# Rows of tokens scattered straight to their expert's place in DRAM, in a fused attention, FFN and top-1 MoE kernel

## The chip, the cores and the metric

One core of a Trainium2 chip runs the whole kernel. The metric is device time in microseconds (us) from start to end of one execution; lower is better. The engines are named as in the profile: PE (matmul; PEld is its weight load), DVE (vector), ACT (scalar), POOL (GpSimd) and SP (which here only issues DMAs and reads registers). ACT and POOL issue some DMAs too. All DMAs run on the core's 16 DMA engines.

## What is computed

Three stages, each feeding the next. 1536 tokens, 512 features.

```
def reference(**kwargs):
    attn_out = _attn_ref(**attn_kwargs)          # 2 x 8 heads x 768 x 64, causal band of 96 + 8 global keys, ALiBi-like bias
    x = np.ascontiguousarray(attn_out.transpose(0, 2, 1, 3)).reshape(B * S, H * D)
    x = _moe_ref(x=x, **moe_kwargs)              # h = x @ w_in (512x2048); (h * sigmoid(h)) @ w_out
    return _moe2_ref(x=x, **moe2_kwargs)

def _moe2_ref(x, w_gate, w_output_gate, w1, w2):
    logits = x @ w_gate                          # 8 experts
    e_idx = np.argmax(logits, axis=1)
    ...                                          # gate_w: softmax probability of the chosen expert
    eom = 1.0 / (1.0 + np.exp(-(x @ w_output_gate)))
    for e in range(E):
        mask = e_idx == e
        h = np.maximum(x[mask] @ w1[e], 0.0)     # 512x1024
        ye = h @ w2[e]                           # 1024x512
        out[mask] = gate_w[mask, None] * eom[mask, e, None] * ye
    return out.astype(np.float32)
```

## The kernel before

The program is ordered by hand: the Python code writes the instructions in the order in which each engine's queue gets them, and each engine runs its own queue in order. P is 128.

**Attention.** The 12 blocks n of 128 queries (6 per batch entry) with 4 head pairs each give 48 slots s. The first 24 slots (n = 0 to 5) run in `slot_b`, fully in float32: per slot `emit_qk` (PE, scores of the next slot), `emit_tb` (DVE, adds the bias and takes the maximum, one instruction per head), `emit_exp` (ACT), `emit_dg` (DVE reciprocals, POOL diagonal matrices), `emit_tr` (PE, the transpose with the scaling, `tp`), `emit_cp` (copy from PSUM, DVE or ACT) and `emit_px` (PE, times v). From slot 8 on a piece of weight decoding (`dec_op`, DVE) stands in each slot. After the last head pair of a block, `emit_xx` calls `put_xt` (L241 to L246): ACT copies the block's result from PSUM to the tile `xT` (rounded, the high part) and DVE writes the difference, the low part, at once. That DVE instruction stands at the end of a slot, ahead of the next slot's `emit_tb`. Slots 0 to 19 and a little more run alone at the program's start; the last of them run inside the first FFN chunk. The loads of the scores' inputs (`ring`) are issued by ACT some four slots ahead, those of v (`vpr`) and of the packed FFN weights (`wiraw`, `woraw`, `wraw`) by SP. Slots 24 to 47 run in `slot`, inside FFN chunks 1 to 3: there POOL makes the low halves `hl` (L176), SP transposes them by DMA (`pT`, L179), and PE multiplies them with v (`pv`, L222).

**FFN.** The tokens go through in five chunks CH=[[0,1],[2],[3],[4],[5]] of token pairs u (256 tokens each), 16 steps each over the hidden features. `s1_mm` (L315) is the first product, `s2_mm` (L335 to L337) the second, two steps later. The low half of the second weight is stored to DRAM in chunk 0 (`wlo_d`, L301) and read again per step in the later chunks (`wolr`, L304).

**Gate.** After a chunk, `s2_ev` puts the 256 rows into `xr` (128 x 2 x 528; 512 features and 16 more columns). `gate1`, `gate2`, `gate3` stand in a list that `run_gates` works off, one entry per FFN step. `gate3(u)` computes each token's place `di` in its expert's list, scatters the token's number there (POOL, L416: two indirect DMAs of 128 x 4 bytes), computes the row's output factor into columns 512 to 527 (DVE reciprocal, L423), and SP stores the 256 rows in token order to the DRAM tensor `XS` (L424). There are two index lists in DRAM, `IX[0]` and, for the last 128 tokens alone, `IX[1]`; `ix_init` fills both with the number of a spare row at the start of chunk 1 (L360 to L368).

**Experts.** `order` ranks the experts by their number of tokens. Expert p of the ranking takes its WIN[p] first places (352 down to 192). The first 128 rows of expert 0 are computed early, in the last FFN chunk: SP reads their index list (`ei`, L494) and POOL gathers the rows (`ex`, `exg`, L499), three indirect DMAs. After the gate, `moe2` runs p = 0 to 7 with 8 steps f each. `load_i` (SP) reads both index lists (`ixt`), `min_i` (DVE) merges them, `load_x` (POOL, L592) gathers the rows (`xw`), `prep_x` transposes them on PE (`xm`, L600); the loop's weights come as `qr` (SP, L480), are split by ACT, DVE and POOL into `uq`, and `put` (POOL, L575) scatters the results to the output, one indirect DMA of 128 rows of 2 KB each.

## Time and profile before

| | us |
|---|---|
| median of 3 runs | 644.12 (639.51 to 645.3) |
| profiled execution, whole | 638.47 |
| its span in the trace | 636.7 |
| PE busy | 594.6 (93%) |
| DVE, ACT, POOL busy | 387.0, 303.3, 208.6 |
| moved by DMA | 99.01 MB (11.61 MB written to DRAM) |
| share of the chain that ended last | PE 69%, DMA 10%, DVE 8%, issue 6%, ACT 4% |

The profiled execution is 0.9% below the median; 1.8 us of its time lie outside the span. Engines' times are busy times within the span. The chain is followed back from the last instruction: each piece is work, or a DMA, that the next piece waited for. PE is busy for most of the span; its idle time and the stretches at a lower granted clock are the rest of the chain.

### The profile page before, as it was taken

The numbers are of one execution on the slowest core, as the hardware profiler recorded it, in microseconds if no ns is written. First come the engines' busy times: TensorE is split into PE (matmuls) and PEld (weight loads), VectorE is DVE, ScalarE is ACT, GpSimd is POOL, SyncE is SP. The second block draws the span as 40 slices with busy tenths as digits, with TensorE's granted clock in tenths as the row PEclk, the third lists the DMA queues.
The fourth block names the chain that finished last, engine by engine and source line by source line (L and its number), as shares of the span: only waits on it lengthen the run. The fifth ranks groups of instructions, "written<-read, shape, count | busy, mean of one in ns | idle before, by whom it ended". The sixth has DMA issues, their size and how long they took to land.

```text
span 636.7 us, 12051 instructions
## 1 busy us (share of the span) xinstructions
PE 594.6 (93%) x4054; PEld 504.1 (79%) x4054; DVE 387.0 (61%) x1060; ACT 303.3 (48%) x802; POOL 208.6 (33%) x248
## 2 busy tenths in 40 slices
PE   2898999999999799999999999998999999999994
PEld 1566788888888588888889998786888888888883
DVE  3577679999546544645463344754835569777740
ACT  5467533343353335343432233744553666676741
POOL 3467614444212242222221001323432434343311
PEclk9999999999999889999999999999799999999998
DMA  7143706774348976485437339715847287578500
GB/s 252 44 129 126 215 34 188 227 218 147 114 142 92 172 160 182 99 165 147 116 91 129 99 80 192 274 35 174 292 148 237 85 283 235 177 244 261 180 18 19
DMA packets 83673, 99.01 MB, mean 156 GB/s; under 512 B 35547, under 2 KB 49883, under 8 KB 83602
## 3 DMA queue, kind: packets, MB, share of 16 engines
q1 hardware_dynamic: 76850, 86.78, 50.0%
q0 software_dynamic: 3312, 8.22, 3.9%
q10 hardware_dynamic: 3440, 3.15, 1.6%
q8 instruction: 34, 0.56, 0.4%
q14 instruction: 37, 0.30, 0.2%
HBM read 82.01 MB, written 11.61 MB: 147 GB/s over the span
## 4 chain that ended last, share of the span: by engine, by line
PE 69%; DMA 10%; DVE 8%; issue 6%; ACT 4%; POOL 2%; SPq 1%; POOLq 0%; DVEq 0%; ACTq 0%
PE s L315 16%; PE s L335 5%; PE s L336 5%; PE s L337 5%; PE h L612 4%; PE tp L193 4%; PE h L618 4%; PE qkp L150 4%; PE y L635 4%; PE y L637 4%; PE y L636 4%; DMA pT<-hl 2%; PE h L613 2%; PE pv L222 2%; PE gl L380 2%
## 5 line engine op out<-in xcount | busy, mean ns | idle before, releaser
L315 PEld LDWEIGHTS s<-xT,wi 128*128 128x128 f32 x1152 | 149.3, 193 | 14.3 <-DVE g L324 7.1
L315 PE MATMUL s<-xT,wi 128*128 128x256 f32 x1152 | 154.1, 286 | 2.6 <-DVE xT L246 1.4
L320 DVE SCALAR_TENSOR_TENSOR s<-u,s 128x256 f32<-128x256 f32 x96 | 39.7, 426 | 88.9 <-ACT u L319 88.9
L319 ACT ACTIVATE u<-s 128x256 f32<-128x256 f32 x96 | 35.2, 380 | 119.5 <-PE s L315 118.9
L335 PE MATMUL s<-woh,g 128*128 128x512 f32 x192 | 79.5, 414 | 0.0
L486 DVE TENSOR_TENSOR uq<-qr,uq 128x512 fp32r<-128x512 f32 x87 | 71.0, 837 | 9.1 <-ACT uq L485 4.4
L336 PE MATMUL s<-woh,g 128*128 128x512 f32 x192 | 76.0, 396 | 0.0
L485 ACT ACTIVATE uq<-qr 128x512 fp32r<-128x512 f32 x112 | 66.7, 626 | 8.3 <-DMA qr<-in_w_dram 7.2
L324 DVE TENSOR_TENSOR g<-s,g 128x256 fp32r<-128x256 f32 x96 | 39.3, 422 | 31.6 <-ACT g L323 28.5
L635 PE MATMUL y<-uq,hh 128*128 128x512 f32 (+6 forms) x136 | 55.7, 409 | 0.0
L323 ACT ACTIVATE g<-s 128x256 fp32r<-128x256 f32 x96 | 35.6, 379 | 40.4 <-DVE s L320 39.4
L637 PE MATMUL y<-uq,hh 128*128 128x512 f32 (+6 forms) x136 | 54.0, 397 | 0.0
L636 PE MATMUL y<-uq,hh 128*128 128x512 f32 (+6 forms) x136 | 53.9, 396 | 0.0
L486 POOL TENSOR_TENSOR uq<-qr,uq 128x512 fp32r<-128x512 f32 x25 | 33.0, 1329 | 52.6 <-ACT uq L485 52.5
L169 ACT ACTIVATE t<-t,mx 128x256 f32<-128x256 f32 (+1 forms) x96 | 45.8, 480 | 6.1 <-DVE mx L162 4.2
L150 PE MATMUL qkp<-ring 64*128 64x256 f32 (+1 forms) x192 | 35.8, 448 | 13.2 <-DMA ring<-in_qk_dram 12.6
L628 DVE SCALAR_TENSOR_TENSOR hh<-h,hh 128x224 fp32r<-128x224 f32 (+6 forms) x64 | 25.3, 395 | 32.8 <-ACT hh L627 29.9
L627 ACT ACTIVATE hh<-h 128x224 fp32r<-128x224 f32 (+6 forms) x64 | 23.2, 363 | 43.4 <-DVE h L625 21.6
L335 PEld LDWEIGHTS s<-woh,g 128*128 128x128 f32 x192 | 36.3, 189 | 7.1 <-ACT u L319 2.0
L337 PE MATMUL s<-wolr,g 128*128 128x512 f32 x128 | 40.5, 398 | 0.0
L336 PEld LDWEIGHTS s<-woh,g 128*128 128x128 f32 x192 | 36.4, 190 | 5.0
L416 POOL DMA_INDIRECT ix<-tok,gdi x12 | 12.4, 1030 | 84.9 <-DVE gsm L420 43.1
(217 smaller groups left out, 1096.7 us busy)
## 6 DMA issues: line engine op xcount, KB each, us to landing
qr<-in_w_dram SPq DMA_DIRECT2D x128, 256.0 KB
wolr<-wlo_d SPq DMA_DIRECT2D x64, 256.0 KB
wiraw<-in_w_in_dram SPq DMA_DIRECT2D x16, 512.0 KB
wraw<-in_w_out_dram SPq DMA_DIRECT2D x13, 512.0 KB
wlo_d<-wol SPq DMA_DIRECT2D x16, 256.0 KB
xs<-xr SPq DMA_DIRECT2D x6, 528.0 KB
ring<-in_qk_dram SPq DMA_DIRECT2D x12, 256.0 KB
ring<-in_qk_dram ACTq DMA_DIRECT2D x10, 256.0 KB
```

The source lines that it names most:

```text
L150: T.matmul(q[:,sl],w[:,z,1],w[:,z:z+1,0] if i==0 else w[:,0:3:2,0] if z==0 else w[:,z-1:z+1,0],start=True,stop=True)
L169: A.activation(out=t[:,j,:ce],in_=t[:,j,:ce],func=AF.Exp,scale=0.125,bias=mx[n][:,h:h+1],accum_out=ss[n][:,h:h+1])
L315: T.matmul(t,w[:,ww,kc,:],x[:,xx,kc,:],start=(k==0),stop=(k==11)); k+=1
L320: V.scalar_tensor_tensor(out=t,in0=u,scalar=1.0,in1=t,op0=ALU.add,op1=ALU.mult)
L335: T.matmul(o,g[u][:,0,sl],wh,start=(f==0),stop=False)
L336: T.matmul(o,g[u][:,1,sl],wh,start=False,stop=False)
L337: else: T.matmul(o,g[u][:,0,sl],wl,start=False,stop=(f==FB-1))
L485: A.activation(out=t[:,0],in_=r,func=AF.Copy)
L486: (G if (i%2 if pool is None else pool) else V).tensor_tensor(out=t[:,1],in0=r,in1=t[:,0],op=ALU.subtract)
L635: T.matmul(o,g[:,0,sl],w[:,0],start=(f==0),stop=False)
L636: T.matmul(o,g[:,1,sl],w[:,0],start=False,stop=False)
L637: T.matmul(o,g[:,0,sl],w[:,1],start=False,stop=(f==7))
```

## The change

- The DRAM tensor `XE` (8 x 1536 rows of 528 floats) replaces `XS` and both index lists. `gate3` writes the token's number into column 513 of its row (POOL copy) and scatters 128 whole rows (2112 bytes each) to their places by an indirect DMA (`gate4(u,0)`). The other 128 rows (`gate4(u,1)`) are an entry of their own in the gate list. All scatters write one tensor, so each waits until the one before it has landed.
- The places that no token takes must hold zeros and the spare number: `rows_init` makes a tile `zr` (POOL), `rows_clear` stores it three times over per expert, eight DMAs of 128 x 3 x 528 floats (811 KB each, 6.5 MB in all), issued by SP after slots 4, 6, ... 18.
- The experts' rows are read by plain SP loads (`load_x`, `xw<-xe`; for the early rows `ex` and `exg`; for expert 0's factors and numbers `xtail`). The index loads, their merging and all 20 gathers by POOL are gone.
- The low part of `xT` for blocks n = 0 to 3 is put in a list (`xlow`) and issued in the next slot, after that slot's reciprocals.
- At the start of `moe2` SP issued the last `xs<-xr`, two `ixt` loads, read the experts' order, two more `ixt` loads, then the `qr` loads; now it reads the order, then issues three `xw<-xe`, `xtail<-xe` and the `qr` loads.
- `run_gates` works off two entries at two places and has one more call in `moe2`, since the list is longer.

```diff
-    XS=dr.tile([NTOK+1,XW],F32,name="xs"); IX=[dr.tile([NE*CAP,1],I32,name=f"ix{k}") for k in range(2)]
+    FAC=512; TOK=513; WROWS=(WIN[0]+P-1)//P*P
+    XE=dr.tile([NE*CAP,XW],F32,name="xe")
...
     def emit_xx(n):
-        put_xt(n,pvt[n])
+        put_xt(n,pvt[n],xlow if 4*(n+2)<SB else None)
...
-    def put_xt(n,m):
+    def put_xt(n,m,later=None):
...
         A.activation(out=sl[:,0],in_=m,func=AF.Copy)
-        V.tensor_tensor(out=sl[:,1],in0=m,in1=sl[:,0],op=ALU.subtract)
+        def low(): V.tensor_tensor(out=sl[:,1],in0=m,in1=sl[:,0],op=ALU.subtract)
+        if later is None: low()
+        else: later.append(low)
...
+    def rows_init():
+        z=mp.tile([P,XW],F32,tag="xT",name="zr",bufs=3); zr.append(z)
         G.memset(z,0.0)
-        S.dma_start(XS[NTOK:NTOK+1,:],z)
+        G.memset(z[:,TOK:TOK+1].bitcast(I32),NTOK)
+    def rows_clear(e):
+        S.dma_start(XE[e*CAP:e*CAP+WROWS,:].rearrange("(a p) d -> p a d",p=P),zr[0][:,None,:].to_broadcast([P,WROWS//P,XW]))
...
-        for t in range(2):
-            n=2*u+t
-            G.indirect_dma_start(out=IX[n==NTT-1][:,:],out_offset=bass.IndirectOffsetOnAxis(ap=di[:,t:t+1],axis=0),in_=tok[:,n:n+1],...)
...
-        S.dma_start(XS[2*u*P:2*(u+1)*P,:].rearrange("(k p) d -> p k d",p=P),xr)
+        G.tensor_copy(xr[:,:,TOK].bitcast(I32),tok[:,2*u:2*u+2])
+        gdi[u]=di,xr
+        gate4(u,0)
+    def gate4(u,t):
+        di,xr=gdi[u]
+        G.indirect_dma_start(out=XE[:,:],out_offset=bass.IndirectOffsetOnAxis(ap=di[:,t:t+1],axis=0),in_=xr[:,t,:],...)
...
+        x=m2['a'].tile([P,XW],F32,name="ex"); ea['x']=x
+        S.dma_start(x,XE[ds(e*CAP,P),:])
         g=mp.tile([P,2,XW],F32,tag="xT",name="exg",bufs=3); ea['xg']=g
+        S.dma_start(g,XE[ds(e*CAP+P,2*P),:].rearrange("(a p) d -> p a d",p=P))
...
+    def load_x(p):
+        small(p); e=ereg(p)
+        for j,n in tiles(p):
+            x=m2['b'].tile([P,XW],F32,tag="xw",name="xw",bufs=6); xwt[p,j]=x
+            S.dma_start(x,XE[ds(e*CAP+j*P,P),:])
...
-        load_i(0); load_i(1)
+        load_x(1); load_t(0)
...
             if o4: emit_px(n4,h4)
+            if xlow: xlow.pop()()
...
+            if s%2==0 and 4<=s<4+2*NE: rows_clear(s//2-2)
...
-                        for fn in (gate2,gate3): gq.append(lambda u=u,fn=fn: fn(u))
+                        for fn in (gate2,gate3,lambda u: gate4(u,1)): gq.append(lambda u=u,fn=fn: fn(u))
```

DVE, the end of block 1 in the attention slots, before. `xT<-px,xT` is the low part, `ISA t,mx` the bias and maximum of a head (a slot has two), `dct<-wiraw,dct` the weight decoding.

```order
L184 TENSOR_SCALAR ss<-ss 128x2
L185 RECIPROCAL ss<-ss 128x2
L246 TENSOR_TENSOR xT<-px,xT 128x4x128
L159 ISA t,mx<-qkp,tabs 128x256
L159 ISA mx 128x1
L271 SCALAR_TENSOR_TENSOR dct<-wiraw,dct 128x512
L159 ISA t,mx<-qkp,tabs 128x256
L159 ISA mx 128x1
L162 TENSOR_SCALAR mx<-mx 128x2
L184 TENSOR_SCALAR ss<-ss 128x2
L185 RECIPROCAL ss<-ss 128x2
```

The same place of the changed kernel:

```order
L186 RECIPROCAL ss<-ss 128x2
L160 ISA t,mx<-qkp,tabs 128x256
L160 ISA mx 128x1
L275 SCALAR_TENSOR_TENSOR dct<-wiraw,dct 128x512
L160 ISA t,mx<-qkp,tabs 128x256
L160 ISA mx 128x1
L163 TENSOR_SCALAR mx<-mx 128x2
L185 TENSOR_SCALAR ss<-ss 128x2
L186 RECIPROCAL ss<-ss 128x2
L248 TENSOR_TENSOR xT<-px,xT 128x4x128
L160 ISA t,mx<-qkp,tabs 128x256
```

The low part moved behind one whole slot's work of DVE; the next slot's first maximum no longer stands behind it.

POOL in chunk 1, the gates of u = 0 and 1, before (`hl` is the low half that SP transposes for PE, `vraw`, `vpr` the split of v):

```order
L176 TENSOR_TENSOR hl<-t,hl 128x2x128 x2
L416 DMA ix_73<-tok,gdi 12288x1 x2
L176 TENSOR_TENSOR hl<-t,hl 128x2x128
L129 TENSOR_TENSOR vraw<-vraw,vpr 128x512
L133 TENSOR_TENSOR vpr<-vraw,vpr 128x512
L176 TENSOR_TENSOR hl<-t,hl 128x2x256
L416 DMA ix_73<-tok,gdi 12288x1 x2
```

and in the changed kernel:

```order
L177 TENSOR_TENSOR hl<-t,hl 128x2x128 x2
L423 COPY xr<-tok 128x2
L429 DMA xe<-xr,gdi 12288x528
L177 TENSOR_TENSOR hl<-t,hl 128x2x128
L429 DMA xe<-xr,gdi 12288x528
L130 TENSOR_TENSOR vraw<-vraw,vpr 128x512
L134 TENSOR_TENSOR vpr<-vraw,vpr 128x512
L177 TENSOR_TENSOR hl<-t,hl 128x2x256 x2
L423 COPY xr<-tok 128x2
L429 DMA xe<-xr,gdi 12288x528
L177 TENSOR_TENSOR hl<-t,hl 128x2x256
L429 DMA xe<-xr,gdi 12288x528
```

One `hl` now stands between the two scatters of a pair; the second still waits for the first to land.

SP at the program's start in the changed kernel, with what each waits for (DMAHW: an earlier DMA that counts on the same semaphore has landed). The `xe<-zr` are the clears; before, the loads stood there without them, two of them in another order.

```order
L260 DMA wiraw<-in_w_in_dram 128x4x256
L370 DMA xe<-zr 128x3x528 [waits DMAHW0_49,Pool_49]
L260 DMA wiraw<-in_w_in_dram 128x4x256 [waits DMAHW2_49]
L370 DMA xe<-zr 128x3x528 [waits DMAHW4_49]
L124 DMA vpr<-in_v_dram 128x512 [waits DMAHW6_49]
L260 DMA wiraw<-in_w_in_dram 128x4x256 [waits DMAHW7_49]
L370 DMA xe<-zr 128x3x528 [waits DMAHW0_49]
L264 DMA woraw<-in_w_out_dram 128x1024 [waits DMAHW2_49]
L370 DMA xe<-zr 128x3x528 [waits DMAHW3_49]
L124 DMA vpr<-in_v_dram 128x512 [waits DMAHW7_49,PE_49,Pool_49]
```

Four clears stand ahead of the fourth v load, which waits for PE; the other four come after it.

## Rows read from the trace of the kernel before

**Rows 1.** The page: PE; the DMA engines' busy tenths in 40 slices.

```profile
PE 594.6 (93%) x4054; PEld 504.1 (79%) x4054; DVE 387.0 (61%) x1060; ACT 303.3 (48%) x802; POOL 208.6 (33%) x248
...
DMA  7143706774348976485437339715847287578500
```

**Rows 2.** Chain that ended last, attention slots: start us, us, what.

```profile
27.77 1.13 PE tp L193 x8
...
31.12 1.13 PE tp L193 x8
...
38.09 1.10 PE tp L193 x8
...
39.87 0.55 ACT xT L245
40.44 0.69 DVE xT L246
41.13 0.33 DVE t L159
...
41.62 1.13 PE tp L193 x8
```

**Rows 3.** Windows: length, busy PE, PEld, DVE, ACT, POOL, PEclk, DMA share, GB/s.

```profile
35.78:38.09 2.31, 2.31 (x21) 1.69 (x21) 1.73 (x9) 1.77 (x8) 1.22 (x3) 1.00 0.41 114
38.09:41.62 3.53, 2.31 (x21) 1.64 (x21) 1.75 (x7) 2.73 (x8) 2.70 (x7) 1.00 0.08 19
41.62:43.97 2.35, 2.35 (x21) 1.73 (x21) 2.28 (x10) 1.41 (x6) 1.55 (x3) 1.00 0.80 281
```

**Rows 4.** Chain at the start, the wait for the scores' inputs.

```profile
8.57 6.31 DMA ring<-in_qk_dram
```

**Rows 5.** DMA from 5 to 17 us: GB/s in 40 slices of 0.3 us.

```profile
GB/s 209 304 345 389 399 376 386 389 382 372 358 355 355 345 352 345 365 352 365 362 355 375 341 386 365 362 399 372 406 338 365 372 358 376 335 369 328 184 113 89
```

**Rows 6.** DMA from 193 to 207 us, slices of 0.35 us: busy tenths, GB/s.

```profile
DMA  0001960999990090009097947093903336525400
GB/s 26 3 0 23 219 133 2 355 362 362 284 66 6 18 18 0 0 0 24 0 12 6 18 30 23 24 35 29 41 0 6 18 29 71 71 53 199 176 7 0
```

**Rows 7.** DMA from 161 to 173 us, slices of 0.3 us, `wlo_d` stores: GB/s.

```profile
GB/s 328 369 382 260 27 0 0 150 410 307 7 0 0 0 0 0 27 0 0 0 0 0 0 314 382 191 7 7 0 0 0 0 0 0 0 0 0 362 389 294
```

**Rows 8.** Output scatters of line 575, 128 rows of 2 KB: landing.

```profile
DMA to landing us min/median/max: 2.8/2.8/3.7
```

**Rows 9.** Waits from 190 to 235 us: total, times, longest.

```profile
POOL ix L416 <- DVE gsm L394: 10.1, 1, 10.1
POOL ix L416 <- DMA ix<-tok,gdi: 9.5, 1, 9.5
...
PE pv L222 <- DMA pT<-hl: 4.6, 3, 2.8
```

**Rows 10.** Windows of FFN steps in chunk 1 (columns as in 3).

```profile
205.39:211.73 6.34, 4.73 (x38) 3.72 (x38) 5.37 (x18) 2.25 (x8) 4.41 (x5) 0.87 0.62 82
...
225.26:230.38 5.12, 5.12 (x44) 4.40 (x44) 1.27 (x5) 2.15 (x7) 1.43 (x2) 0.81 0.65 68
230.38:234.60 4.22, 4.12 (x43) 3.34 (x42) 2.81 (x11) 2.15 (x7) 1.17 (x2) 1.00 1.12 329
```

**Rows 11.** PE's waits for DMAs, 395 to 456 us.

```profile
PE xm L600 <- DMA xw<-xs,ixt: 3.0, 1, 3.0
PE em L514 <- DMA ex<-xs,ei: 1.6, 1, 1.6
```

**Rows 12.** Chain, from the last gate to expert 1's rows.

```profile
425.86 7.31 DMA ix<-tok,gdi
...
439.76 6.65 DMA xw<-xs,ixt
```

**Rows 13.** Windows behind that wait (columns as in 3).

```profile
445.00:450.00 5.00, 3.54 (x11) 2.80 (x12) 4.83 (x16) 2.86 (x7) 3.83 (x4) 0.57 0.99 378
450.00:455.00 5.00, 5.00 (x23) 4.43 (x22) 3.38 (x8) 2.45 (x6) 1.29 (x1) 0.75 0.78 200
```

More of the change, by code (lines that the diff above doesn't have):

```diff
@@ L359, in gate_consts @@
         S.dma_start(wgs,wg.rearrange("(k p) e -> p k e",p=P))
-    def ix_init():
-        n=NE*CAP//P
-        z=mp.tile([P,n],I32,tag="stage",name="zi",bufs=2)
-        G.memset(z,NTOK)
-        for x in IX: S.dma_start(x.rearrange("(p a) o -> p (a o)",p=P),z)
-        z=mp.tile([1,XW],F32,tag="stage",name="zx",bufs=2)
+    zr=[]
+    def rows_init():
+        z=mp.tile([P,XW],F32,tag="xT",name="zr",bufs=3); zr.append(z)
         G.memset(z,0.0)
-        S.dma_start(XS[NTOK:NTOK+1,:],z)
+        G.memset(z[:,TOK:TOK+1].bitcast(I32),NTOK)
+    def rows_clear(e):
+        S.dma_start(XE[e*CAP:e*CAP+WROWS,:].rearrange("(a p) d -> p a d",p=P),zr[0][:,None,:].to_broadcast([P,WROWS//P,XW]))
     def gate1(n):
@@ L423, in gate3 @@
         V.reciprocal(out=xr[:,:,512:XW],in_=s[:,:,29:30].to_broadcast([P,2,XW-512]))
-        S.dma_start(XS[2*u*P:2*(u+1)*P,:].rearrange("(k p) d -> p k d",p=P),xr)
+        G.tensor_copy(xr[:,:,TOK].bitcast(I32),tok[:,2*u:2*u+2])
+        gdi[u]=di,xr
+        gate4(u,0)
+    gdi={}
+    def gate4(u,t):
+        di,xr=gdi[u]
+        G.indirect_dma_start(out=XE[:,:],out_offset=bass.IndirectOffsetOnAxis(ap=di[:,t:t+1],axis=0),in_=xr[:,t,:],in_offset=None,bounds_check=NE*CAP-1,oob_is_err=False)
     def order(c):
@@ L491, in early_load @@
     def early_load():
-        e=ereg(0); nt=(WIN[0]+P-1)//P
-        i=m2['a'].tile([P,nt],I32,name="ei"); ea['i']=i
-        S.dma_start(i,IX[0][ds(e*CAP,nt*P),:].rearrange("(a p) o -> p (a o)",p=P))
-        ea['x']=m2['a'].tile([P,XW],F32,name="ex")
+        e=ereg(0)
+        x=m2['a'].tile([P,XW],F32,name="ex"); ea['x']=x
+        S.dma_start(x,XE[ds(e*CAP,P),:])
         g=mp.tile([P,2,XW],F32,tag="xT",name="exg",bufs=3); ea['xg']=g
-        G.memset(g,0.0)
-        for j in range(nt):
-            G.indirect_dma_start(out=g[:,j-1] if j else ea['x'],out_offset=None,in_=XS[0:NTOK-2*P,:],in_offset=bass.IndirectOffsetOnAxis(ap=i[:,j:j+1],axis=0),bounds_check=NTOK-2*P-1,oob_is_err=False)
+        S.dma_start(g,XE[ds(e*CAP+P,2*P),:].rearrange("(a p) d -> p a d",p=P))
     def early_iota():
@@ L581, in paired, with small, load_t, tail @@
     def paired(p): return WIN[p]-R0[p]<PAIR
-    def load_i(p):
-        W=WIN[p]; nt=(W+P-1)//P; e=ereg(p)
-        t=m2['b'].tile([P,2,3],I32,tag="ix",name="ixt",bufs=4); ixt[p]=t
-        for k in range(2): S.dma_start(t[:,k,:nt],IX[k][ds(e*CAP,nt*P),:].rearrange("(a p) o -> p (a o)",p=P))
+    def small(p):
+        ixt[p]=m2['b'].tile([P,3],I32,tag="ix",name="ixt",bufs=4)
         sct[p]=m2['b'].tile([P,3],F32,tag="sc",name="sc",bufs=4)
-    def min_i(p):
-        t=ixt[p]; nt=(WIN[p]+P-1)//P
-        V.tensor_tensor(out=t[:,0,:nt],in0=t[:,0,:nt],in1=t[:,1,:nt],op=ALU.min)
-    def load_x(p,j):
-        x=m2['b'].tile([P,XW],F32,tag="xw",name="xw",bufs=6); xwt[p,j]=x
-        G.indirect_dma_start(out=x,out_offset=None,in_=XS[:,:],in_offset=bass.IndirectOffsetOnAxis(ap=ixt[p][:,0,j:j+1],axis=0),bounds_check=NTOK,oob_is_err=False)
+    def load_x(p):
[3 more added lines that the diff above has]
+            S.dma_start(x,XE[ds(e*CAP+j*P,P),:])
+    def load_t(p):
+        small(p); e=ereg(p); j,k=tiles(p)[0][0],len(tiles(p))
+        x=m2['b'].tile([P,k,XW-FAC],F32,name="xtail"); xwt[p]=x
+        S.dma_start(x,XE[ds(e*CAP+j*P,k*P),FAC:XW].rearrange("(a p) d -> p a d",p=P))
+    def tail(p,j,f,i):
+        V.tensor_copy(sct[p][:,j:j+1],f)
+        V.tensor_copy(ixt[p][:,j:j+1],i.bitcast(I32))
     def prep_x(p,j):
@@ L603, in prep_x @@
         V.tensor_tensor(out=lo,in0=m[:,:,:n],in1=hi,op=ALU.subtract)
-        V.tensor_copy(sct[p][:,j:j+1],x[:,512:513])
-    def fac_x(p,j):
-        V.tensor_copy(sct[p][:,j:j+1],xwt.pop((p,j))[:,512:513])
+        tail(p,j,x[:,FAC:FAC+1],x[:,TOK:TOK+1])
     h1={}; hh={}; yp={}
@@ L689, in moe2 @@
                 f1_ev(p,f,spl if ns else lambda: None)
-                if g in (1,2):
-                    min_i(2-g)
-                    for j,n in tiles(2-g): load_x(2-g,j)
                 if p+1<NE:
@@ L695, in moe2 @@
                     while nq[0]<min(16,nq[1]+4*(f+1),nq[1]+NQR): load_u(4*(p+1)+nq[0]//4,nq[0]%4); nq[0]+=1
-                    if p and f==0:
-                        for j,n in tiles(p+1): load_x(p+1,j)
+                    if p and f==0: load_x(p+1)
                     if p==0 and f==5:
-                        for j,n in tiles(0): fac_x(0,j)
-                    if f==2 and p+2<NE: load_i(p+2)
-                    if f==5 and p+2<NE: min_i(p+2)
+                        for k,(j,n) in enumerate(tiles(0)): tail(0,j,xwt[0][:,k,0:1],xwt[0][:,k,1:2])
                     t=tiles(p+1)
@@ L983 @@
                     w_to(1,0,g+2); w_to(2,1,g-1); w_to(1,1,g)
-                if g==FB:
-                    load_v(SB//4)
-                    ix_init()
-                if g>=LAG+FB: run_gates(2 if g==(len(CH)-1)*FB+2 else 1)
+                if g==FB: load_v(SB//4)
+                if g>=LAG+FB: run_gates(2 if g-(len(CH)-1)*FB in (2,4) else 1)
             if g>=LAG:
```

8 lines of the change are left out of this document (5 added, 3 removed).

## The prediction

> **What bounds the kernel now.** I read the page first, then the chain that ended last, then the waits and windows of the places where the chain leaves PE. The page shows PE busy for 594.6 us, 93% of the span, with no other engine over 61% [rows 1]. So there are some 42 us in which PE idles, and a little more in which its granted clock is low. A change that touches only DMA, DVE and POOL gains where it takes such a place off the chain. Five places come up, in program order.
>
> The attention slots repeat every 2.31 us with PE busy throughout [rows 3]. At the end of a block the distance between two groups of `tp` matmuls is larger: 31.12 - 27.77 = 3.35 us for block 0, 41.62 - 38.09 = 3.53 us for block 1 [rows 2], and the latter comes twice more, for blocks 2 and 3. The chain says why: ACT's copy to `xT`, then DVE's low part (0.69 us), then the first bias instruction of the next slot (0.33 us), and only then PE. That bias instruction needs nothing of `xT`; it is late because it stands behind it in DVE's queue.
>
> In chunk 1 of the FFN, POOL waits 9.5 us for the landing of its own scatter of numbers, and 10.1 us in another wait that the trace puts down to DVE; in the same stretch PE waits 4.6 us for `pT`, which comes out of the `hl` that stand behind the scatters on POOL [rows 9]. Four FFN steps from 205.39 to 230.38 take 24.99 us, the next one 4.22 us; the granted clock is 0.87 in the first and 0.81 in the last of the four [rows 10].
>
> In the last chunk PE waits 1.6 us for the early rows, and at the start of the expert loop 3.0 us for expert 1's rows [rows 11]. The latter is the end of a chain of DMAs: scatter of numbers 7.31 us, reading them back, gather 6.65 us [rows 12]. Behind it the granted clock is 0.57 and 0.75 for 5 us each [rows 13].
>
> **The change, part by part.** All sums are against the profiled execution, 638.5 us.
>
> *The low part of `xT`, a slot later.* The excess is 1.04 us once and 1.22 us three times, 4.7 us in all [rows 2, 3]. With the instruction behind the next slot's work, the bias instruction can run as soon as its scores exist, and these are computed one slot ahead. DVE has room: the slot before the boundary, the boundary and the one after hold 1.73 + 1.75 + 2.28 = 5.76 us of DVE work, with the low part in it, and three periods are 6.93 us [rows 3]. ACT has 1.77 + 2.73 + 1.41 = 5.91 us. The slot that now gets the 0.69 us holds 2.97 us, 0.66 us over the period; DVE can start it early, since the boundary slot is left with 1.06 us of work. I take 4.4 us; the ends are 4.7, and 0 if the crowded slot makes the following `tp` late by as much.
>
> *The eight clears.* POOL's two fills of `zr` lie at the start, where it has nothing else to do. Each clear moves 811 KB. The first two are issued by SP ahead of loads that it issued at once before, at about the time of the `ring` load that PE waits for: issued at 8.57, landed 6.31 us later [rows 4]. From 5 to 16 us the DMA engines already move 340 to 400 GB/s throughout [rows 5], so 811 KB cost 2.2 us of that stretch each. The load order shows what stands back for them: the second and third weight loads, 512 KB each, and the third v load now wait for earlier landings. Two clears less two 512 KB loads is 0.6 MB, 1.6 us; one clear less two loads is below nothing. I take 1.0 us of delay, ends 0 and 2.6 us (a third load not held back). The other six fall between 15 and 62 us, where the DMA engines' share is 1, 4 and 3 tenths in a slice [rows 1]; 6 x 2.2 = 13 us more of 47 is covered, as `ring` is loaded four slots, 9 us, ahead. If that cover were gone, each late `ring` would cost up to 2.2 us.
>
> The Trainium skill speaks against this part ("DMA: Bandwidth & Descriptors", section "Issuing engines are not separate DMA queues"): transfers started by different engines run on the same 16 DMA engines and interleave. By that rule alone both clears, 4.5 us, would stand beside ACT's `ring` load and the sum would be 3.5 us worse; the rows agree that these engines are full there, and what decides is which loads are held back, which only the changed trace can show.
>
> *Chunk 1.* The scatter of numbers and the store of `xr` beside it go; a scatter of 128 rows of 2112 bytes takes their place. The nearest row is the output scatter, 128 rows of 2048 bytes, which lands in 2.8 us, at most 3.7 [rows 8]. So POOL's second scatter waits about 3 us instead of 9.5, and one `hl` runs in between. Of 24.99 us four undisturbed steps would leave 4 x 4.22 = 16.9; 8.1 us are in question [rows 10]. Some of these steps do work that was late from before, and 3 us of waiting on POOL remain, so I take 5 us; the ends are 0 and 8.1.
>
> *The early rows.* SP reads them directly where it read the list and POOL gathered. One landing instead of two: the 1.6 us go [rows 11]; ends 0 and 1.6.
>
> *Into the expert loop.* The last two scatters now go one after the other and must wait for the reciprocal. From about 426.2, two landings of 2.8 to 3.7 us end at 431.8 to 433.6; plain loads, even as slow as the gather's 6.65 us, are there at 438.5 to 440.3. PE came to need them at 446.4 - 3.0 = 443.4 [rows 11, 12]. So the 3.0 us go, and what the clock lost behind them: 3.54 us at 0.57 and 5.00 us at 0.75 are 5.8 us of work in 8.5 us, 2.8 us [rows 13]. I take 5.0 of 5.8 us. The other end: both scatters take the 7.31 us of the scatter of numbers [rows 12]; then the rows come at about 447.5, and with the `qr` loads queued behind them on SP it is 1.5 us worse than before.
>
> *The rest* costs nothing I can place: in the later experts POOL loses two gathers per expert and DVE gains a copy of one column per tile, both off PE's chain; if POOL bounded there, it would be a gain. The gate entry that moves one step later lies inside PE-bound steps.
>
> Sum: 4.4 - 1.0 + 5.0 + 1.6 + 5.0 = 15.0 us, 638.5 - 15.0 = 623.5 us. The median before, 644.1, is 0.9% above its profiled execution; by the same ratio the median after is **629 us**.
>
> **The rivals**, in terms of that median.
>
> *Half of it comes back.* The DMA share is 0.99 and 0.78 where the expert loop starts [rows 13]: with the rows earlier, PE may next wait for weights instead, and keep 1 us of the 5. In chunk 1 the transposes may still be 3 us late behind each scatter, which leaves 2 of 5. Gain 4.4 - 1.0 + 2 + 1.6 + 1 = 8 us: 636 us.
>
> *Row scatters are slow.* If in these stretches a row scatter lands as late as the scatter of numbers (7.31 us or more), chunk 1 gains nothing and the expert loop starts 1.5 us later: 4.4 - 1.0 + 0 + 1.6 - 1.5 = 3.5 us, 641 us. For it: they go to places strewn over 26 MB of DRAM. Against it: so do the output's rows over their tensor, in 2.8 us [rows 8].
>
> *Slower: the clears clog the DMA engines.* The store of `xr`, also rows of 2112 bytes, moved at 355 to 362 GB/s for 1.4 us from 195.5, and then the engines stood at 0.9 busy with some 20 GB/s until 205 [rows 6]. If rows of that size do this, each of the first two clears holds the `ring` load for up to 8 us, and later pairs do it again. With 8 to 16 us at the start, no gain in chunk 1 and 1.5 us lost at the expert loop, the result is 3.5 to 11.5 us slower, more with the later pairs: 654 us as a middle. It decides the sign once `ring` comes over 4.5 us later than before. Against it: the stores of `wlo_d`, rows of 2048 bytes, went through at 300 to 410 GB/s and left nothing behind [rows 7]; what was different at 195 us is that a scatter of 4-byte numbers ran beside the store. The rows cannot separate the two, but the number scatter is the odder one.
>
> Beside this stands a line of the Trainium skill ("DMA: Bandwidth & Descriptors", section "Specifications"): transfers under 512 bytes lead to a read-modify-write. By it the 4-byte scatter would be the one that clogs, both would vanish with the change, and the time would be that of the forecast; no row here shows a number scatter alone.
>
> **How the numbers follow.** Chances: forecast 0.52, half comes back 0.20, slow row scatters 0.13, clogging clears 0.15. A measurement of this kernel can tell about 1% (6.4 us) from no change. The first two are faster by more than that, except a small part of the second: 0.70. The third, with that part, is within 1%: 0.15. Slower: 0.15. The range runs from 619, where chunk 1 gives 8.1 and the rest its full size with a bit more at the start, to 646, which holds the third rival and the edge of the fourth; it leaves out most of the fourth. The likeliest case by itself spans 624 to 634.
>
> **What would show it.** In the changed trace: `tp` 2.31 us apart over all block ends; PE's first wait for `ring` at most 2 us longer; clears that move over 300 GB/s with no tail of a busy engine at 20 GB/s; POOL's wait for a row scatter near 3 us, and four steps in chunk 1 near 20 us; no wait of PE for `ex` or `xw`, and a full clock at 445 to 455 us of before. The prediction is wrong if row scatters or clears show tails of 5 us or more, or if PE waits at the same places for weights.

## The result, and the profile after

The changed kernel takes 619.6 us (median of 4 runs, 616.87 to 621.69) where the kernel before takes 641.8 (4 runs, 637.22 to 645.3): a ratio of 0.9656, 95% interval 0.9573 to 0.9738. Its profiled execution takes 621.69 us with a span of 620.0, against 638.47 and 636.7: 16.8 us less, 0.974. Timed again beside the last experiments, the same kernel took 620.75 us (6 runs) where the kernel before took 635.11 (11 runs, 630.62 to 640.37): 0.9783, interval 0.9742 to 0.9824. One of these 11, the 640.37, ran in a slow state and is left out of the ratio. So the gain is 22 us by the first medians and 14 by the second. The kernel before varies by some 15 us over all its runs, the changed one by 6, so the two traces, step against step, say more than the medians do.

The page after: PE, and the DMA engines' busy tenths [rows 1].

```profile
PE 590.6 (95%) x4054; PEld 500.6 (81%) x4054; DVE 389.1 (63%) x1069; ACT 303.0 (49%) x802; POOL 186.2 (30%) x233
...
DMA  7639725674355587465444327607845378569500
```

PE has the same 4054 matmuls and is busy 4.0 us less; its mean granted clock on record is 0.999 where it was 0.987. The idle 42 us have become 29. The same matmuls in both traces, by the time at which they start, show where the difference arises:

| place | before, us | after, us | difference |
|---|---|---|---|
| first group of `tp` of the attention | 17.57 | 17.77 | +0.2 |
| first FFN step | 72.04 | 72.26 | +0.2 |
| first of the four steps in chunk 1 | 205.23 | 203.12 | -2.1 |
| the step behind them | 230.22 | 222.08 | -8.1 |
| last step of the last FFN chunk | 409.12 | 398.14 | -11.0 |
| fourth pair of second products of expert 0 | 452.72 | 435.75 | -17.0 |
| seventh pair | 461.60 | 446.90 | -14.7 |
| last second product | 627.70 | 613.04 | -14.7 |
| end of the span | 636.7 | 620.0 | -16.7 |

So the attention gains nothing, chunk 1 gives 8.3, chunk 3 gives 0.3, the early rows 2.6, the start of the expert loop 6.0, of which 2.3 are given back at once, the experts nothing, and the last microseconds, after all work is done, 2.0.

**Attention.** A block end of the chain after, as [rows 2] before (start us, us, what):

```profile
49.92 1.10 PE tp L194 x8
51.11 0.56 ACT pT L199
51.71 0.55 ACTq L121
52.30 1.10 ACT t L170 x4
53.43 0.20 DVE ss L185
53.65 0.17 DVE ss L186
53.82 0.59 DVE xT L248
54.41 0.33 DVE t L160
...
55.57 1.09 PE tp L194 x8
```

The low part is off the place it stood in, but it is on the chain again: ACT's two copies (the second, to `xT`, runs from 51.65 to 52.25, while ACT also issues the `ring` load that the chain names), then the exponentials, then DVE's sum and reciprocal that wait for these, then the low part, then the bias instruction of the slot after. And the start:

```profile
8.21 8.28 DMA ring<-in_qk_dram
```

This load is not the one of [rows 4]: that was the fourth, and this is the fifth, for the second block. PE's two groups of `qkp` that use the fourth and the fifth, before and after (start us, us, what; in brackets PE's idle time and what ended it):

```profile
15.02 0.80 PE L150 MATMUL qkp<-ring 64*128 64x128 f32 x4 [4.40 <-DMA ring<-in_qk_dram]
16.42 1.23 PE L150 MATMUL qkp<-ring 64*128 64x256 f32 x4 [0.59 <-DVE mx L159]
```

```profile
14.02 0.80 PE L151 MATMUL qkp<-ring 64*128 64x128 f32 x4 [3.46 <-DMA ring<-in_qk_dram]
16.62 1.23 PE L151 MATMUL qkp<-ring 64*128 64x256 f32 x4 [1.80 <-DMA ring<-in_qk_dram]
```

The fourth load comes a microsecond earlier than before (ACT issues it at 7.83 instead of 8.57), and the fifth makes PE start 0.2 us later than before.

**Chunk 1.** The number scatters' place is taken by row scatters. POOL's wait in 190 to 225 us, and the landing of all twelve:

```profile
POOL xe L429 <- DMA xe<-xr,gdi: 3.5, 2, 2.8
```

```profile
DMA to landing us min/median/max: 2.8/3.5/5.0
```

The four steps as one window (columns as in [rows 10]):

```profile
203.28:222.24 18.96, 18.96 (x187) 16.08 (x186) 12.24 (x54) 9.35 (x31) 7.52 (x8) 1.00 0.58 141
```

18.96 us instead of 24.99, PE busy throughout and the clock at 1.00. These four steps hold 187 matmuls where the same four before held 170, since the longer gate list moves the second pair's gate one step on; the -2.1 us of the table at their start is mostly this shift. The whole chunk has the same 581 matmuls in both, and takes 77.4 us before and 69.1 after, from its first step to that of chunk 2.

**Start of the expert loop.** The chain after, in the place of [rows 12]:

```profile
418.72 2.99 DMA xe<-xr,gdi
422.08 0.35 SPq L591
...
425.39 5.43 DMA qr<-in_w_dram
430.85 0.64 ACT uq L490
...
434.64 1.19 DVE cntf L453
...
437.67 0.40 DVE hh L632
438.11 1.08 PE h L616 x4
```

No wait of PE for `ex` or `xw` is left, and the clock stays at 1.00 in the windows that answer [rows 13]:

```profile
433.00:438.00 5.00, 4.38 (x24) 3.33 (x22) 4.78 (x18) 2.96 (x8) 1.30 (x1) 1.00 0.90 304
438.00:443.00 5.00, 4.89 (x28) 4.19 (x29) 4.40 (x15) 4.39 (x11) 1.29 (x1) 1.00 0.65 211
```

But DVE is busy for 4.78 of 5 us there: it has become the engine that is waited for. `cntf` (L453) is the first of `flags`, eleven instructions of DVE that work out a flag which is read after the last expert; they stand from 434.56 to 436.85 us, the first of them 1.27 us long.

### The profile page after: what moved, and what is told of

It reads as the page before. It is cut to its first block, busy times and chain, and to the rows that moved or that the text cites. A ratio compares the mean times of both kernels' runs of the same rounds, so it can differ in the third digit from the quotient of the medians.

```text
span 620.0 us, 12009 instructions
## 1 busy us (share of the span) xinstructions
PE 590.6 (95%) x4054; PEld 500.6 (81%) x4054; DVE 389.1 (63%) x1069; ACT 303.0 (49%) x802; POOL 186.2 (30%) x233
## 4 chain that ended last, share of the span: by engine, by line
PE 69%; issue 8%; DVE 8%; DMA 6%; ACT 4%; POOL 3%; SPq 1%; ACTq 0%; POOLq 0%; DVEq 0%
PE s L319 17%; PE s L339 6%; PE s L340 5%; PE s L341 5%; PE h L616 5%; PE h L622 4%; PE qkp L151 4%; PE y L639 4%; PE y L641 4%; PE y L640 4%; PE tp L194 3%; PE h L617 2%; POOL wol L303 2%; PE pv L224 2%; PE gl L382 1%
## 5 line engine op out<-in xcount | busy, mean ns | idle before, releaser
L319 PEld LDWEIGHTS s<-xT,wi 128*128 128x128 f32 x1152 | 147.3, 190 | 13.1 <-DVE g L328 6.0
L319 PE MATMUL s<-xT,wi 128*128 128x256 f32 x1152 | 152.2, 284 | 1.9 <-DVE xT L248 1.4
L632 DVE SCALAR_TENSOR_TENSOR hh<-h,hh 128x224 fp32r<-128x224 f32 (+6 forms) x64 | 25.3, 395 | 31.8 <-ACT hh L631 31.8
L577 POOL DMA_INDIRECT out_dram<-y,ixt x17 | 17.4, 1024 | 74.9 <-ACT y L646 56.7
```

The source lines that it names most:

```text
L319: T.matmul(t,w[:,ww,kc,:],x[:,xx,kc,:],start=(k==0),stop=(k==11)); k+=1
```

## The experiments

Unless said otherwise an experiment is one profiled execution, read by the start times of the same matmuls as in the table above; such a reading repeats to about 0.1 us from one step to the next, while the attention's first 35 us differ from run to run (below). e10 is the changed kernel run again, and e6, e7 and e12 are the same program up to chunk 1; with the first execution that makes five, and they reach the first FFN step at 70.61 to 73.01 us.

**e1, the low part back in its place**, all else as changed.

```diff
-        put_xt(n,pvt[n],xlow if 4*(n+2)<SB else None)
+        put_xt(n,pvt[n])
```

> The changed kernel with the low part of xT at once again, as in the kernel before; all else stays. The result's trace puts the gain of moving it at 1.5 us between the seventh and the nineteenth group of tp matmuls (33.79 us before, 32.24 after), not 4.4. If that is the move's whole worth, this stretch takes 33.8 us again and the kernel loses 1.5 us against the changed one. If the move also costs the 1.6 us that the changed kernel loses ahead of that stretch, at the first block end, then that loss vanishes here and the kernel ends level with the changed one. If the move were worth the 4.4 us of the prediction and something else eats it, the kernel loses over 4 us.

The kernel takes 622.92 us, the changed one 621.69. The seventh and the nineteenth group of `tp` stand at 33.19 and 65.11, 31.92 us apart; in the changed kernel at 35.17 and 65.11, 29.94 apart, and before 31.49. (The 33.79 and 32.24 of the expectation run to the twentieth group, by a slip in counting.) So the move is worth 1.6 to 2.0 us in that stretch, since e1 waits 0.4 us for `ring` at its end. The block ends of blocks 1 to 3 lie in this stretch. The stretch before it, from the first group to the seventh, takes 15.2 us here and 17.4 in the changed kernel, so both meet at 65.11; in e7 and e12, which have the move, it takes 15.5, so the move alone does not make it long. The 1.2 us by which e1 is slower arise elsewhere, at the start of the expert loop: its last row scatter lands 4.99 us after its issue instead of 2.99, and PE is 1.3 us later by the fourth pair of second products. The end of the attention's chain shows another thing:

```profile
55.55 8.79 DMA ring<-in_qk_dram
64.34 0.14 issue
64.48 0.70 PE qkp L151 x4
```

A `ring` load that is four slots ahead of its use lands 8.79 us after its issue, since two clears and two weight loads were issued just ahead of it. The cover of the later clears is thin.

**e2, the clears later.**

```diff
+    CLR=(8,9,10,12,13,14,16,17)
...
-        rows_init()
         s=0
         while s<SB:
+            if s==3: rows_init()
...
-            if s%2==0 and 4<=s<4+2*NE: rows_clear(s//2-2)
+            if s in CLR: rows_clear(CLR.index(s))
```

> The changed kernel with zr filled at slot 3 and the clears issued after slots 8, 9, 10, 12, 13, 14, 16, 17 instead of 4, 6, ... 18; all else stays. Theory: the first clears delay the ring load by 1.6 us, and PE, started later, gets its full rate one slot later, which costs the 1.6 us at the first block end. Then here the ring load lands near 14.9, the fourth group of tp takes 0.7 instead of 1.2 us, and everything behind is 1.5 to 1.8 us earlier than in the changed kernel. Rival: the loss comes with the moved low part; then nothing changes by more than 0.4 us. Third: six clears in 42 to 62 us are too many, and ring loads there come late; then PE waits for ring there.

619.19 us, 2.5 less than the changed kernel. The first group of `tp` is 1.36 us earlier (16.42), so the first clears do delay the start. This is no measure against the kernel before, which e2 leads by 1.15 us at the same place: there `woraw` (512 KB) is issued at 7.91 us, here at 16.65. The first FFN step is 1.67 us earlier than in the changed kernel's first execution, but level with its second (e10: 70.61, here 70.58), which is 1.46 later at the first group: what e2 saves at the start it loses between 49 and 54 us, where PE waits 1.2 us for DVE's weight decoding (`dct`). The third possibility of the expectation comes in part: a `ring` load lands at 62.66, 7.61 us after its issue, and PE waits 0.5 us for it. The second half of the theory fell: the fourth group of `tp` still took 1.22 us for four matmuls although PE had started earlier. When PE comes to its full rate differs between executions of one and the same program. The fourth and fifth group of the kernel before (start us, us, what; four or eight matmuls):

```profile
25.84 0.71 PE L193 MATMUL tp<-dg,t 128*128 128x128 f32 x4
27.77 1.13 PE L193 MATMUL tp<-dg,t 128*128 128x128 f32 x8 [0.21 <-DVE mx L159]
```

of the changed kernel:

```profile
26.05 1.22 PE L194 MATMUL tp<-dg,t 128*128 128x128 f32 x4
28.98 2.08 PE L194 MATMUL tp<-dg,t 128*128 128x128 f32 x8
```

and of the changed kernel run again (e10):

```profile
26.15 1.22 PE L194 MATMUL tp<-dg,t 128*128 128x128 f32 x4
28.89 1.16 PE L194 MATMUL tp<-dg,t 128*128 128x128 f32 x8
```

Four matmuls take 1.22 us at the lower rate and 0.71 at the higher. In these three the rate has risen by 25.8, only after the group that begins at 28.98, and by 28.9 us. In e3 and e4, which are the kernel before up to 170 us, the group at 25.85 is still slow, and they are 0.9 us behind the kernel before at the first FFN step. e10 reaches the first FFN step at 70.61, 1.65 us ahead of the first execution of the same kernel. So up to that much of what the changed kernel lost in its attention is this, and not the change, unless the change itself shifts the moment, which three executions of the old start (the kernel before, e3, e4) cannot rule out.

**e3 and e4: which of the two DMAs of the gate is slow.** The kernel before without the stores of `xr`, and without the scatters of numbers.

```diff
# e3
-        S.dma_start(XS[2*u*P:2*(u+1)*P,:].rearrange("(k p) d -> p k d",p=P),xr)
+        S.dma_start(XS[0:NTOK,:].rearrange("(a p) d -> p a d",p=P),z[:,None,:].to_broadcast([P,NTT,XW]))   # once, in ix_init
# e4
-            G.indirect_dma_start(out=IX[n==NTT-1][:,:],...,in_=tok[:,n:n+1],...)
```

> The kernel before without the six stores of xr to DRAM (the rows are stored as zeros once, at the start of chunk 1, so that the gathers have something to read; the output is therefore not the reference's). The scatters of 4-byte numbers stay. Theory N, the number scatters clog: POOL still waits some 9 us at each pair in chunk 1, and the four steps that took 24.99 us before still take near 25 us. Theory R, the rows of 2112 bytes clog: POOL waits about 3 us, and the four steps take 17 to 19 us.

> The kernel before without the twelve scatters of token numbers (the index lists keep their fill, so all gathers read the spare row or nothing; the output is not the reference's). The stores of xr stay. Theory N: a store of 540 KB is through in about 1.5 us and leaves no tail of busy engines at 20 GB/s; the four steps in chunk 1 take 17 to 19 us. Theory R: the tail of some 8 us stays behind each store, with wolr reads stuck in it.

In e3 the four steps take 22.35 us with the clock at 0.85, and POOL issues its second number scatter 10.2 us after the first (203.83, 213.99). In e4 they take 17.18 us.

```profile
215.79:238.14 22.35, 19.86 (x170) 16.49 (x170) 11.83 (x48) 8.47 (x29) 8.34 (x8) 0.85 0.73 144
```

```profile
206.19:223.37 17.18, 17.18 (x170) 14.23 (x170) 10.30 (x45) 8.24 (x29) 5.37 (x5) 1.00 0.63 152
```

The first is e3, the second e4. DMA from 193 to 207 us of e4 (GB/s in slices of 0.35 us), with one store of `xr` in it, against [rows 6]:

```profile
GB/s 249 334 62 0 0 0 178 188 8 264 362 344 326 187 100 381 288 51 230 141 22 94 271 351 263 383 328 375 190 12 0 0 177 219 203 174 141 140 380 65
```

The store is through in some 1.5 us, and what comes behind it moves at up to 383 GB/s. So theory N holds: the scatter of 4-byte numbers holds things up, and the stores of rows without it do not. (e3's 22.35 us lie 2.6 below the kernel before's 24.99, so beside the numbers the stores may add to it.) e3 is 10.4 us late before these steps, which is the price of storing 3.2 MB of zeros just ahead of chunk 1; its steps are compared with one another alone. e4 is also 10.9 us ahead at the end of the last FFN chunk and 14.6 at the last product, both against its own first FFN step: nearly all that the changed kernel gains, with the index lists, the gathers and the row stores still there. Place by place it is the changed kernel: chunk 1 takes 69.0 us (there 69.1), the last chunk to its last step 45.7 (45.7), and from there to the fourth pair of second products 37.6 (37.6). That is an upper bound on what the numbers alone cost, since in e4 the gathers read one spare row over and over and the output scatters write nothing.

**e5, the reciprocals a slot later**, on the changed kernel.

```diff
-            if o1: emit_dg(n1,h1)
+            if 0<=s-2<SB: emit_dg(*divmod(s-2,4))
```

> The changed kernel with emit_dg (DVE's sum and reciprocal, POOL's diagonal matrices) for slot s - 2 instead of s - 1; the transpose needs them for s - 3, so nothing is late. Theory: the moved low part stands behind reciprocals that wait for ACT's exponentials (ACT's copies of pT and xT are ahead of these at a block end), so the next slot's bias instruction is still late there, which leaves 0.9 to 1.0 us at a block end. With the reciprocals of an older slot DVE waits for nothing; the three distances of 3.2 to 3.3 us between groups of tp become 2.3 to 2.6, and the stretch from the seventh to the nineteenth group takes 29.5 to 30.5 us instead of 32.2. Rival: DVE simply has too much to do in the slot that gets the low part (2.97 us); then 2.8 us or more stays at each block end and the gain is under 1 us.

622.62 us, 0.9 slower. The block ends do what the theory says in part: 42.87 to 45.47 is 2.60 (3.17 in the changed kernel), 62.67 to 65.06 is 2.39 (2.69), but 52.52 to 55.75 is 3.23 (3.34), and the stretch takes 29.12 us where the changed kernel's takes 29.94 (the 32.2 of the expectation again runs to the twentieth group). A gain of 0.8 us is what the rival allowed, so the two are not told apart. What is late next shows in PE's waits from 28 to 75 us:

```profile
PE s L319 <- DVE xT L248: 1.4, 1, 1.4
PE tp L194 <- POOL dg L188: 1.0, 2, 0.8
PE qkp L151 <- DVE ss L186: 0.8, 1, 0.8
```

The diagonal matrices now come too late for PE now and then, and in the first FFN chunk, where the last slots run between steps, the later order costs 1.5 us for good.

**e6, the flags later**, on the changed kernel.

```diff
-                if g==4: flags()
+                if g==20: flags()
```

> The changed kernel with flags() in step 20 of the expert loop instead of step 4. Theory: with the rows there early, DVE bounds the first steps (short ones, of 224 columns, beside the splits of the next weights); the trace shows flags() on DVE from 434.56 to 436.85, ahead of splits and evictions, and 2.3 us of the 6.0 gained at the start of the loop are given back between 436 and 447. Then 1 to 2.3 us come back here at 447 and stay to the end. Rival: the weights' loads set the pace of these steps; then under 0.5 us changes.

620.03 us. At the seventh pair of second products it is 2.02 us ahead of the changed kernel, and no PE wait is left from 430 to 448 us; where the flags now stand, in step 20, 0.8 goes again, 0.5 comes back by 540 us (as in e1 and e8 to e11, so it is the changed kernel's first execution that loses it), and at the last product it is 1.7 ahead. The bound at the loop's start is DVE, as the theory says: eleven instructions that nothing there needs.

**e7, number scatters put back** into a tensor that nothing reads, on the changed kernel.

```diff
+        for t in range(2): G.indirect_dma_start(out=IXD[:,:],out_offset=bass.IndirectOffsetOnAxis(ap=di[:,t:t+1],axis=0),in_=tok[:,2*u+t:2*u+t+1],...)
```

> The changed kernel with the twelve scatters of 4-byte numbers put back, into a DRAM tensor that nothing reads; all else stays. Theory N (the number scatters alone clog): chunk 1 loses the 8 us again, and POOL waits 9 us at a number scatter. Rival: they clogged only beside the row store; then a number scatter is through in about 3 us and chunk 1 loses 3 us or less.

655.72 us: 34 us slower than the changed kernel, and slower than the kernel before. DMA from 194 to 214 us, and PE's wait from 190 to 245:

```profile
DMA  0482893968600010000000000095091903999999
GB/s 0 99 163 38 111 86 37 49 37 37 37 0 16 20 41 8 16 8 8 4 4 0 0 1 0 0 329 211 14 216 33 94 4 135 397 365 379 325 143 337
...
ixd<-tok,gdi POOLq DMA_INDIRECT x2, 10.0
xe<-xr,gdi POOLq DMA_INDIRECT x2, 5.1
```

```profile
PE pv L225 <- DMA pT<-hl: 9.9, 3, 5.0
```

From 197 us to the landing of the first number scatter at 203.8 the DMA engines move under 50 GB/s, and in most of that time they do not even read as busy. The scatters of numbers whose landing the trace has take 3.9 to 10.0 us, longest in chunk 1. The loss in chunk 1 is 17 us, twice the 8 of the kernel before; here the row scatters stand behind the numbers on POOL, and no run separates the two.

**e8, three edits together** (e2, e5 and e6).

> The changed kernel with all three edits: clears later (worth 2.6 us when tried alone), dg a slot later (1.5 to 2.5 us expected) and flags later (1 to 2.3 us expected). If the three add up, the profiled execution takes 614.5 to 617 us where the changed kernel's took 621.7; if the DMA queue, full from 50 to 64 us with clears, is what bounds the end of the attention slots, dg later adds nothing on top of the clears and it takes 617 to 618.

618.65 us, above both expected ranges (614.5 to 617, or 617 to 618). The first FFN step is 2.47 us early, of which the rest of the first chunk takes 1.5 as in e5, and one `ring` load lands late among the clears:

```profile
44.64 7.99 DMA ring<-in_qk_dram
52.64 0.14 issue
```

**e9, the three mended by that trace**: `emit_dg` one slot later only up to slot 19, four clears ahead of the fourth v load, flags in the last expert.

```diff
-            if o1: emit_dg(n1,h1)
+            for r in ((s-2,) if s<20 else (s-2,s-1) if s==20 else (s-1,)):
+                if 0<=r<SB: emit_dg(*divmod(r,4))
...
-                if g==4: flags()
+                if g==57: flags()
...
-        rows_init()
+            if s==3: rows_init()
...
-            if s%2==0 and 4<=s<4+2*NE: rows_clear(s//2-2)
+            for e,x in enumerate(CLR):     # CLR=(8,9,10,10,12,13,16,17)
+                if x==s: rows_clear(e)
```

> The three edits of e8 mended by its trace: dg for slot s - 2 only up to slot 19 (both at slot 20, then s - 1 as before), since e5 and e8 lose 1.5 us in the first FFN chunk, where the last slots run; four clears ahead of the fourth v load and two in the next block (e8 had three and three), since a ring load issued at 44.64 landed after 7.99 us there; flags() in step 57, the last expert, where nothing is split. Expected against the changed kernel's steps: 2.5 to 3.3 us earlier at the first FFN step, the same at the end of chunk 0, 2 us more at the start of the expert loop with none given back: 616 to 617.5 us. If the fourth early clear delays an early ring load, the first FFN step is under 2 us earlier.

616.86 us. The first FFN step is 2.11 us early, under the 2.5 expected, and so is the end of chunk 0, the seventh pair of second products is 4.40 us early, the last product 4.91. Of this, the 2.3 us between the fourth pair and the seventh are those of the flags; in the last expert they cost nothing.

**e10 and e11, the changed kernel and that of e9, timed together.**

> The changed kernel itself, timed beside the kernel before and beside the next one on one chip. By its first times 0.966 of the kernel before; by the profiled executions 0.974. Expected 0.965 to 0.975.

> The kernel of e9 timed. Its trace is 4.9 us ahead of the changed kernel's at the last expert's steps, 0.8%; expected 0.957 to 0.967 of the kernel before, and 3 to 6 us under the changed kernel's median. If what e9 won lies in one execution's start alone (the step at which PE runs at its full rate differs from run to run), it is under 2 us.

620.75 us (618.4 to 622.42, ratio 0.9783, 0.9742 to 0.9824) and 617.91 us (617.0 to 618.53, ratio 0.9741, 0.9704 to 0.9777). The medians are 2.8 us apart, 0.46%, and all but one of the six runs of the first lie above all six of the second; the two intervals against the kernel before overlap. Both ratios lie above what was expected, and e11's gain on the changed kernel just under it. e11's own trace shows why 4.9 us were too many: PE came to its full rate late in this execution (eight matmuls from 28.22 take 2.07 us), its first FFN step is only 0.2 us ahead of the changed kernel's first execution, and 3.3 us are left at the last product, 2.2 of them from the flags. So a gain at the start is not shown, the flags' is. e10's trace gains 1.6 us in the attention and loses it between 430 and 436 us. Its last row scatter lands after 4.63 us, at 422.25; the changed kernel's first execution has it after 2.99, at 421.71, although PE is 1.3 us later there. Row reads, `qr`, its split and the flags follow in both. In e1 it was the same. So the start of the loop hangs on this landing: in seven of the nine executions with 30 indirect DMAs it takes 2.7 to 3.0 us, in these two 4.6 and 5.0.

**e12, scatters of 64 bytes** instead of the 4 of e7, into records of their own.

```diff
+        for t in range(2): G.indirect_dma_start(out=IXD[:,:],...,in_=xr[:,t,512:528],...)   # IXD: 8 x 1536 records of 16 floats
```

> The changed kernel with twelve scatters more, as in e7 into a tensor that nothing reads, but of 64 bytes per token instead of 4 (columns 512 to 527 of the row, into a list of 64-byte records). If the shortness of the pieces clogs, whatever their place, 64 bytes land in 5 to 10 us too and chunk 1 loses 5 us or more. If it is that neighbouring numbers of 4 bytes fall into the same stretch of DRAM, 64-byte records, each in its own, land in about 3 us and chunk 1 loses 2 to 4 us, for two more landings that POOL waits for.

635.66 us, 14 us slower than the changed kernel, 20 less than e7. From 194 to 214 us:

```profile
ixd<-xr,gdi POOLq DMA_INDIRECT x2, 4.1
xe<-xr,gdi POOLq DMA_INDIRECT x2, 3.7
```

A scatter of 64-byte records lands in 4.1 us where that of 4-byte numbers took 10.0, and chunk 1 loses 3.3 us, as the second theory had it. The rest lies at the early rows (6.5) and at the start of the expert loop, where four scatters in a row stand on POOL instead of two. So short pieces as such are not what takes 10 us. Whether it is the 4 bytes or the neighbourhood of the numbers in one list is open: the records change both.

## Why the prediction was right, point by point

The median lies at the low edge of the range, and the sign and the main mechanisms were right: 15.0 us were expected between the profiled executions, 16.8 came. But the sum is right by errors that cancel. And the median is 9.4 us under the 629 forecast, of which the sum has 1.8: the rest is the step from a profiled execution to a median, which was 0.9% up before and is 0.3% down after.

*The low part, 4.4 taken, 2.2 to 2.6 measured.* e1 gives 1.6 to 2.0 for three of the four block ends; at the first, from the fifth group of `tp` to the seventh, it is 5.06 us in e10 against 5.63 before, 0.6 more. The step that failed is the sentence that the bias instruction can run as soon as its scores exist. That holds for the slot right behind the block end. The next slot's bias instruction stands behind the reciprocals and now behind the low part too, and the reciprocals wait for ACT's exponentials, which at a block end come after ACT's two copies. I had DVE's and ACT's busy times, which fit, but not the order between them. The lower end, a crowded slot that makes the next `tp` late, was named and partly came. e5 speaks for this order without settling it: with older reciprocals two of the block ends shrink by 0.6 and 0.3 us, the third by 0.1.

*The clears, 1.0 taken, 0.2 measured against the kernel before.* Clears and held-back loads nearly cancel: without the early clears the start is 1.4 us earlier (e2), but that order also holds `woraw` back and leads the kernel before by 1.15. That the loads held back decide was foreseen; the term was too large. And the prediction watched one `ring` load, that of [rows 4], which comes earlier; the next one is what PE now starts late by. In this stretch, the two first slices aside, over 300 GB/s move, and no tail follows: by 27 us the engines read as idle. GB/s from 5 to 17 us, where [rows 5] stood.

```profile
GB/s 181 290 349 400 399 376 386 393 382 372 365 360 369 395 395 390 394 380 383 353 307 312 345 318 346 399 381 402 386 404 415 397 394 397 412 401 379 394 389 386
```

The rival in which they clog is therefore out. One reading behind that rival was off: in [rows 6] the engines do not stand at 0.9 busy until 205 us, the slices change between 0 and 0.9. What failed is a part of the cover: with clears the engines are nearly full from 50 to 64 us as well, and a `ring` load four slots ahead is no longer safe there (e1, e2, e8; in e7, which is the changed kernel up to chunk 1, PE waits 1.8 us for it before 63.67 us). Set against the low part the attention should have come out 2 us ahead; e10 is 1.4 ahead at the first FFN step, the first execution 0.2 behind. From the third group of `tp` to the seventh that execution lost 1.6 us, although the block end in it gained 0.6, so some 2.1 us (an estimate from these) are PE's late full rate.

*Chunk 1, 5 taken, 8.3 measured.* The mechanism was right, the term too small. I kept 3 us back for POOL's remaining wait. That wait is there (2.8 and 0.7 us), but an `hl` runs in it, and PE has no wait left in the stretch. The upper end of 8.1 was about right. e3, e4 and e7 show the cause that the prediction left open between two: it is the scatter of numbers. The rule of the Trainium skill that stood beside that rival ("DMA: Bandwidth & Descriptors", section "Specifications": under 512 bytes a read-modify-write) pointed the right way for the 4-byte numbers; no run shows the read-modify-write itself, and 64-byte records, also under that size, land in 4.1 us (e12), so by itself it does not give the size.

*The early rows, 1.6 taken, 2.6 measured.* Besides PE's one wait, the steps around it had lost another microsecond, which went with it.

*Into the expert loop, 5.0 taken, 3.7 measured.* 6.0 us came, all that was in question, and 2.3 went again in the next ten. The rival in which half comes back was right that something takes the place of the rows, and wrong about what: the 2.3 us are not the weights' loads, but DVE with the flags in its way (e6). The weights' loads do stand on the chain ahead of that, by a new order on SP: the first `qr` loads are issued after the row reads, which wait for the last scatter. Where that scatter lands late (e1, e10), another 1.3 to 1.6 us go; so the rival of slow row scatters comes true here in two of nine executions, in small. Loading `qr` ahead of the rows was not tried.

*The end, nothing taken, 2.0 measured.* This term was missing: the prediction put the rest at nothing it could place; see below.

## What to carry to other kernels

Price a scattered write by what it does to all other transfers in flight, not by its bytes: 128 numbers of 4 bytes took up to 10 us during which the other transfers hardly moved, 128 whole rows of 2 KB landed in 2.8 to 5.0 us in the changed kernel, and PE waited for nothing beside them in chunk 1. Before a large change, take out alone what is suspected: e4, without the number scatters, gains 14.6 us between the first FFN step and the last product, the whole change 14.9. When an instruction is moved behind others on its engine, follow for two slots what these others wait for, since busy times that fit say nothing about an order that doesn't. And when a wait goes, look for work that nobody needs at that place; here moving eleven instructions gave 2.0 to 2.3 us at the loop's start, and all of it stayed once they stood in the last expert (e9, e11).

## What the runs showed of the hardware that was not expected

*The end of the program takes longer in the executions whose POOL has issued more indirect DMAs.* POOL's last drain, after all work (the longest of three), before and after:

```profile
L1044 POOLq DRAIN  x3: 40/107/4162, 631.7 to 636.4; - x3
```

```profile
L1044 POOLq DRAIN  x3: 40/107/2529, 616.6 to 619.7; - x3
```

From the issue of the last output scatter to the end of the span it takes 7.13 us with 50 indirect DMAs in the program (the kernel before; e3 7.15), 6.33 and 6.38 with 42 (e7, e12), 5.62 with 38 (e4) and 5.09 or 5.10 with 30 (the changed kernel and the eight other executions with as many). That is 0.07 to 0.1 us for each. These fourteen executions go with the count, but that it is the cause is not shown: no run varied it alone.

*For PE's first microseconds the trace has no granted clock.* A window of the kernel before (columns as in [rows 3]):

```profile
16.00:32.00 16.00, 14.09 (x72) 8.82 (x72) 9.48 (x47) 7.94 (x31) 6.53 (x14) 1.00 0.16 44
```

The window prints 1.00, the level of 2.4 GHz, and yet four matmuls of the same kind take 1.22 us at 23 and 0.71 at 26. The trace's first record of the clock stands at 25.8 us in the kernel before, at 31.8 in the changed kernel and at 28.6 in e10, and gives full clock from there on; a stretch without a record is printed as 1.00. These are also the moments at which the matmuls become short. In e7 the clock is on record as 0.5, the level of 1.2 GHz, from 64.35 to 67.76 us, and eight `tp` matmuls take 2.07 us there, as long as the eight at 28.98 in the changed kernel:

```profile
64.31 2.07 PE L195 MATMUL tp<-dg,t 128*128 128x128 f32 x8
```

```profile
64.35:66.38 2.03, 2.03 (x11) 1.81 (x12) 1.60 (x7) 0.00 (x0) 1.18 (x2) 0.50 0.67 236
```

So the time before the first record was most likely spent at that level. PE had waited for `ring`, or for DVE behind it, until 15 to 17 us in all of these executions; after that the first record comes between 24.2 us (e1) and 33.1 (e6), differently in executions of one program.
